# Transposing u in two row groups of 64 tokens, each into its own PSUM bank

## The chip, the cores and the metric

The kernel runs on one core of a Trainium2 chip. The metric is the device time of one execution in microseconds (us); lower is better. Three executions of the kernel before took 1543.83, 1544.32 and 1544.84 us, so the median is 1544.32 us. The core has five engines that run side by side, each through its own queue in order: TensorE (PE in the profile; its weight loads have a row of their own, PEld), VectorE (DVE), ScalarE (ACT), GpSimd (POOL) and SyncE (SP), which here only issues DMAs. TensorE writes its results to PSUM, which the kernel uses as eight banks of 128 partitions by 512 float32 numbers: four banks hold two tiles `ph` of 128 x 1024, and four more are handed out one by one as `px`.

## The reference

An attention through 49 agents is followed by a feed-forward block with SoLU and a layer norm. The second stage takes nearly all of the time:

```python
a2k = sm(agents, k); agent_v = a2k @ v        # per batch, 4 batches of 12608 tokens, 128 channels
x = sm(q, agents) @ agent_v                   # (50432, 128)
h = x @ w_in                                  # (50432, 1024)
e = exp(h - max(h)); sm = e / (sum(e) + 1e-9)
solu = h * sm
ln = (solu - mean(solu)) / sqrt(var(solu) + 1e-6) * g_ln
out = ln @ w_out                              # (50432, 128)
```

## The kernel before

**Tiles.** The tokens go through in n = 396 tiles of 128 (x counts them, 99 to a batch), in groups G of four. For each tile the kernel computes h for 128 tokens x 1024 features in `ph` (`c_h`, line 756, four matmuls: two feature halves, each with a high and a low part of the combined weights), its maximum over the features on VectorE (`c_max`, line 760), the exponential on ScalarE (`c_exp`, line 770), and u = h * exp on VectorE (`c_u`, line 775). ScalarE also sums the squares (`c_sq`, line 781) for the variance. The scale of a token is worked out on GpSimd, sent round through DRAM and multiplied in at the very end (`c_rstd`, `c_fin`).

**The turn.** The second matrix product needs u with features on the partitions, so TensorE transposes it. `c_t` (line 784) does it in two calls to a tile, one for each half of the features (hf = 0, 1), and each takes one px bank: four transposes of a 128 x 128 block (u is the loaded operand, the identity the streamed one) fill 128 features x 512 numbers. The names in the profile are `px<-ident,u`. `c_ev` (line 799) evicts each half on ScalarE: into `uT` in SBUF, or, for the halves that `DIR` names (`direct`), straight into the rounded high part `uH`. From uT, GpSimd makes uH (`c_sph`, line 814) and the low rest `uL` (`c_spl`, line 818), with one instruction over 1024 columns where neither half is direct, and over 512 where one is. For a direct half VectorE makes uL from the bank itself (`c_ldir`, line 809), and the bank comes free after that.

**The second product.** `c_w` (line 836) takes two tiles together (256 tokens): 24 matmuls of 256 columns accumulate in half a px bank, three for each of the eight feature blocks kf (wH with uH, wH with uL, wL with uH). One bank holds two such pairs until `c_fin` reads it. The first matmuls, up to half of the 24, waited for the parts of the first feature half only, those behind for both.

**Side stages.** Each batch begins with the agents' attention over the keys (`phase_a`), and every eighth tile with the queries' (`phase_b`). Some of their matmuls fill only 64 of the array's columns: lines 427 and 476 (`phase_a`) and 656 (`phase_b`) write to px partitions 0 to 63 and 64 to 127 in turns. Line 500 has an operand of one row.

**The order.** At build time a planner (`Plan.run`) places every operation in a list schedule: each has an engine, a booked cost, a due time and what it depends on. An operation with `take` can only start when a px bank is free by the plan; the one named by `free` gives it back. On TensorE the table `SWITCH` books a cost between kinds of operations: kind 2 are the ones with 64 columns, 0 the large products, 1 the rest. The order in which the planner calls the operations is the order of each engine's instructions. On the chip an engine goes through that order and waits by semaphores, so the booked costs do not set the time, but they set the order. Due times such as DT, DEV, DLD, DSP and DW (lines 177 to 181) are constants, counted in tiles.

Of the kernel before, what the change touches and what calls it, by code (L numbers as in the profile page):

```python
# [9 lines left out]
F32 = mybir.dt.float32  # L10
# [4 lines left out]
ALU = mybir.AluOpType  # L15
# [10 lines left out]
class Plan:  # L26
# [5 lines left out]
           "AA": 0.0, "AG": 0.17, "GP": 0.25 + MARGIN, "GD": 0.1, "GG": 0.1, "GA": 0.2}  # L32
    EPS = {"P": 0.01, "A": 0, "D": 0.07, "G": 2.6, "S": 0.0}

    SWITCH = ((0.0, 0.0, 0.09), (0.0, 0.0, 0.09), (0.15, 0.12, 0.0))

    HOLD = 0.12

# [7 lines left out]
    def op(self, eng, fn, cost, due, deps=(), take=False, free=None, after=(), kind=1, shy=0.0):  # L46
        o = Op()
        o.kind, o.shy = kind, shy
        o.eng, o.fn, o.cost, o.due, o.take, o.free = eng, fn, cost, due, take, free
        o.deps, o.outs, o.end, o.bank = [d for d in deps if d is not None], [], None, None  # L50
        o.left = 0
        for d in o.deps + [d for d in after if d is not None]:
            if d.end is None:
                o.left += 1
                d.outs.append(o)
        if not o.left:
            self.push(o)
        return o
# [7 lines left out]
    def run(self, idle=None):  # L66
        while True:
            best = None
            for e, ops in self.cand.items():
                if not ops:  # L70
                    continue
                free = [b[0] for b in self.banks if b[0] is not None]
                first = min(free) if free else None
                at, opts, low = self.at[e], [], None
                for o in ops:
                    s = max(at, o.ready[e])
                    if o.take:
                        if first is None:
                            continue
                        s = max(s, first)  # L80
                    opts.append((s, o))
                    low = s if low is None else min(low, s)
                if low is None:
                    continue
                near = [z for z in opts if z[0] <= low + self.EPS[e]]
                if e == "P" and self.kind == 2:
                    near = [z for z in opts if z[0] <= low + self.HOLD and z[1].kind == 2] or near
                s, o = min(near, key=lambda z: z[1].due)
                if o.shy > 0.0:
                    s, o = min((z for z in opts if z[0] <= s + o.shy), key=lambda z: z[1].due)  # L90
                if best is None or s < best[0]:
                    best = (s, e, o)
            if best is None:
                break
            s, e, o = best
            for z in o.eng:
                self.cand[z].remove(o)
            if o.take:
                can = [b for b in self.banks if b[0] is not None and b[0] <= s]
                bank = max(can, key=lambda b: b[0])  # L100
                bank[0], o.bank = None, bank
            if idle is not None and e == "P":
                idle(s - self.at[e])
            o.start, o.by = s, e
            if e == "S":
                hold, size, lag = o.cost
                self.at[e] = s + hold
                if size:
                    self.dma = max(self.dma, s + 2.0) + size / 0.36
                    o.end = self.dma + 0.3  # L110
                else:
                    o.end = s + lag
            else:
                c = o.cost[o.eng.index(e)] if len(o.eng) > 1 else o.cost
                if e == "P":
                    c += self.SWITCH[self.kind][o.kind]
                    self.kind = o.kind
                o.end = self.at[e] = s + c
            if o.free is not None:
                o.free.bank[0] = o.end + self.LAT[e + "P"]  # L120
            if o.fn:
                args = [o.bank[1]] if o.take else []
                if len(o.eng) > 1:
                    args.append(e)
                o.fn(*args)
            for z in o.outs:
                z.left -= 1
                if not z.left:
                    self.push(z)
# [3 lines left out]
def kernel(  # L133
# [11 lines left out]
    nc = tc.nc  # L145
# [3 lines left out]
    P = 128  # L149
    NF = DF // P  # L150
# [5 lines left out]
    AP2 = 64  # L156
# [3 lines left out]
    DIR = {(1, 0), (1, 1), (3, 1), (5, 1), (7, 1)}  # L160
    LGC = 8
    UB = 8
    TD = 2
    WC = 4

# [11 lines left out]
    DT = -0.42  # L177
    DEV = 5.19
    DLD = 0.41
# [601 lines left out]
        nc.scalar.activation(out=sq, in_=u, func=AF.Square, bias=su, scale=-float(DF),  # L781
                             accum_out=st[G]["Q"][:, j : j + 1])

    def c_t(x, hf, pt):
        rr[x, hf] = pt
        for kf in range(4):
            k0 = hf * 4 + kf
            nc.tensor.transpose(pt[:, kf * P : (kf + 1) * P], us[x][0][:, k0 * P : (k0 + 1) * P], ident)  # L788

    def direct(x, hf):  # L790
        return (x % (2 * GT), hf) in DIR or x >= n - TD

    def parts(x, k0, k1):
        i, j = divmod(x, 2)
        if i not in pr:
            pr[i] = [gpool.tile([P, NF, 2 * P], F32R, tag=t, name=f"{t}{x}") for t in ("uH", "uL")]
        return [t[:, k0:k1, j * P : (j + 1) * P] for t in pr[i]]

    def c_ev(x, hf):
        uH, _ = parts(x, hf * 4, hf * 4 + 4)  # L800
        pt = rr[x, hf].rearrange("p (k t) -> p k t", t=P)
        if direct(x, hf):
            nc.scalar.copy(out=uH, in_=pt)  # L803
        else:
            if x not in rr:
                rr[x] = epool.tile([P, NF, P], F32, tag="uT", bufs=UTB, name=f"uT{x}")
            nc.scalar.copy(out=rr[x][:, hf * 4 : hf * 4 + 4, :], in_=pt)  # L807

    def c_ldir(x, hf):
        uH, uL = parts(x, hf * 4, hf * 4 + 4)  # L810
        pt = rr[x, hf].rearrange("p (k t) -> p k t", t=P)
        nc.vector.tensor_tensor(out=uL, in0=pt, in1=uH.bitcast(F32), op=ALU.subtract)  # L812

    def c_sph(x, k0, k1):
        uH, _ = parts(x, k0, k1)
        nc.gpsimd.tensor_scalar(out=uH, in0=rr[x][:, k0:k1, :], scalar1=1.0, scalar2=0.0, op0=ALU.mult, op1=ALU.add)  # L816

    def c_spl(x, k0, k1):
        uH, uL = parts(x, k0, k1)
        nc.gpsimd.tensor_tensor(out=uL, in0=rr[x][:, k0:k1, :], in1=uH.bitcast(F32), op=ALU.subtract)  # L820

    WM = 3 * NF

# [95 lines left out]
    def F(f, *x):  # L919
        return lambda *y: f(*x, *y)  # L920
# [30 lines left out]
    def at(x, d, r, l):  # L951
        return x + d + (r * (1.0 - x / 12.0) if x < 12 else l if x >= (B - 1) * TB else 0.0)
# [4 lines left out]
    for x in range(n):  # L957
# [18 lines left out]
        if len(dh) < 2:  # L976
            utl.append(x)
            if len(utl) > UTB:
                buf.append(SP[utl[-1 - UTB]])
            if len(utl) <= UTB:  # L980
                buf += wready if (len(utl) + 2) % UTB == 2 else cout
        for hf in range(2):
            T[x, hf] = op("P", F(c_t, x, hf), 0.435, at(x, DT, DTR, DTL) + 0.02 * hf, [U[x]] + buf, take=True)
            EV[x, hf] = op("A", F(c_ev, x, hf), 0.477, at(x, DEV, DEVR, DEVL) + 0.02 * hf, [T[x, hf]],
                           free=None if hf in dh else T[x, hf])
            if hf in dh:
                LD[x, hf] = op("D", F(c_ldir, x, hf), 0.602, at(x, DLD, DLDR, DLDL), [EV[x, hf]], free=T[x, hf])
        need = [[LD.get((x, hf)), EV[x, hf]] for hf in range(2)]
        if len(dh) < 2:
            k0, k1 = (4 if 0 in dh else 0), (4 if 1 in dh else NF)  # L990
            SH[x] = op("G", F(c_sph, x, k0, k1), 0.17 + 0.107 * (k1 - k0), at(x, DSP, DSPR, DSPL),
                       [EV[x, hf] for hf in range(2) if hf not in dh])
            SP[x] = op("G", F(c_spl, x, k0, k1), 0.16 + 0.268 * (k1 - k0), at(x, DSP, DSPR, DSPL) + 0.02, [SH[x]])
            for hf in range(2):
                if hf not in dh:
                    need[hf] += [SH[x], SP[x]]
        else:
            SP[x] = None
        need_prev = need if x % 2 == 0 else [need_prev[hf] + need[hf] for hf in range(2)]
        if x % 2 == 1:  # L1000
            prev = None
            for m0 in range(0, WM, WC):
                m1 = min(m0 + WC, WM)
                lead = m0 == 0 and (i % 2 == 0 or i == n // 2 - 1)
                f = (lambda px, i=i, m1=m1: c_w(i, 0, m1, px)) if lead else F(c_w, i, m0, m1)
                o = op("P", f, 0.1192 * (m1 - m0), at(x, DW, DWR, DWL) + 2.0 * m0 / WM,
                       need_prev[0] + (need_prev[1] if m1 > WM // 2 else []) + wready + [prev, W.get((i - 1, 1)), FIN.get(G - 2)], take=lead, kind=0)
                if lead:
                    pol.append(o)
                prev = o  # L1010
            W[i, 1] = prev
# [75 lines left out]
```

## Time and profile before

| | |
|---|---|
| executions, us | 1543.83, 1544.32, 1544.84 |
| median, us | 1544.32 |
| profiled execution, us | 1545.92 |
| its span, first to last instruction, us | 1544.1 |
| instructions in the trace | 35,508 |
| granted TensorE clock, mean | 0.995 |
| HBM traffic, GB/s over the span | 85 |

The profile is that of one execution. Its page has the busy time of each engine, the chain of work that ended last, and the costliest groups of instructions; views of the trace give single instructions in order of time. In a group's row stand the line of the kernel, the engine, the operation, output and inputs by name, their shapes and the number of instructions, then the busy time in us, the mean time of one in ns, and the idle time of the engine before them. The span covers all but 1.8 us of the profiled execution, and that execution was 1.6 us over the median of the three.

### The profile page before, as it was taken

To read this page: it belongs to the slowest core of one execution; us is meant where nothing else is said; L and a number is where in the kernel's file an instruction comes from. 1 tells how busy PE (TensorE), PEld (TensorE's weight loads), DVE (VectorE), ACT (ScalarE), POOL (GpSimd) and SP (SyncE) were. 2 spreads that over 40 slices of the span, in tenths; PEclk is the share of its full clock that TensorE was granted. 3 is DMA by queue.
4 is the path that set the end of the run, shared out by engine and by line. 5 is a ranking of instruction groups with operands and counts; after the bars stand their busy time and mean duration, and the time that the engine had idled before them with its cause. 6 is when DMAs were issued, how large, how long until landed. Compare 5 with 4: busy or idle time off the path is not lost.

```text
span 1544.1 us, 35508 instructions
## 1 busy us (share of the span) xinstructions
PE 1514.7 (98%) x12624; PEld 1356.7 (88%) x12624; DVE 1373.8 (89%) x2213; ACT 1421.5 (92%) x2739; POOL 1256.1 (81%) x1613
## 2 busy tenths in 40 slices
PE   8799999999999999999999999999999999999998
PEld 5589898898898888999898998989999999999988
DVE  6889988898999888998989988888989989999896
ACT  3589999999999999999999999999999999999996
POOL 1478888788887888778877798888888989998986
PEclk9999999999999999999999999999999999999999
DMA  9533323333324342423234332432232323231211
GB/s 373 171 111 116 122 85 112 106 87 108 92 72 152 104 121 90 139 80 106 83 93 133 105 122 85 127 99 91 81 90 59 85 69 90 71 88 54 63 56 46
DMA packets 114720, 159.65 MB, mean 103 GB/s; under 512 B 16240, under 2 KB 71152, under 8 KB 114544
## 3 DMA queue, kind: packets, MB, share of 16 engines
q1 hardware_dynamic: 114544, 157.39, 32.9%
q8 instruction: 100, 1.64, 0.4%
q14 instruction: 76, 0.62, 0.1%
HBM read 105.36 MB, written 26.02 MB: 85 GB/s over the span
## 4 chain that ended last, share of the span: by engine, by line
PE 71%; ACT 9%; DVE 8%; POOL 5%; issue 4%; DMA 2%; SPq 0%; DVEq 0%; ACTq 0%; POOLq 0%
PE px L836 27%; PE ph L756 18%; PE px L788 16%; ACT e L770 3%; PE px L476 2%; DVE u L775 2%; PE px L427 2%; ACT sq L781 2%; POOL uL L820 2%; PE px L656 2%; ACT uT L807 2%; DVE nm L760 1%; DMA pT<-pn 1%; POOL uH L816 1%; PE px L460 1%
## 5 line engine op out<-in xcount | busy, mean ns | idle before, releaser
L820 POOL TENSOR_TENSOR uL<-uT,uH 128x1024 fp32r<-128x1024 f32 (+1 forms) x344 | 662.4, 1926 | 25.4
L760 DVE TENSOR_REDUCE nm<-ph 128x1 f32<-128x1024 f32 x396 | 479.5, 1216 | 69.2 <-PE ph L756 67.7
L775 DVE SCALAR_TENSOR_TENSOR u<-ph,e 128x1024 f32<-128x1024 f32 x396 | 481.1, 1219 | 38.3 <-ACT e L770 27.1
L781 ACT ACTIVATE sq<-u,su 128x1024 bf16<-128x1024 f32 x396 | 463.2, 1170 | 29.8 <-DVE u L775 22.2
L770 ACT ACTIVATE e<-ph,nm 128x1024 f32<-128x1024 f32 x396 | 448.8, 1137 | 19.2 <-DVE nm L760 18.0
L836 PE MATMUL px<-uL,wH 128*128 128x256 f32 x1584 | 462.8, 292 | 0.0
L836 PE MATMUL px<-uH,wH 128*128 128x256 f32 x1584 | 451.1, 285 | 2.6 <-ACT uT L807 1.3
L836 PE MATMUL px<-uH,wL 128*128 128x256 f32 x1584 | 449.8, 284 | 0.0
L788 PE MATMUL px<-ident,u 128*128 128x128 f32 x3168 | 431.5, 274 | 8.5 <-DVE u L775 7.4
L788 PEld LDWEIGHTS px<-ident,u 128*128 128x128 f32 x3168 | 366.2, 141 | 45.2 <-DVE u L775 7.2
L756 PE MATMUL ph<-mh,pT 128*128 128x512 f32 x792 | 335.3, 423 | 5.2 <-DMA pT<-pn 2.8
L816 POOL TENSOR_SCALAR uH<-uT 128x1024 fp32r<-128x1024 f32 (+1 forms) x344 | 299.9, 872 | 32.3 <-ACT uT L807 30.2
L756 PE MATMUL ph<-ml,pT 128*128 128x512 f32 x792 | 313.8, 396 | 0.2 <-DVE ml L552 0.2
L836 PEld LDWEIGHTS px<-uH,wH 128*128 128x128 f32 x1584 | 299.0, 189 | 16.1 <-issue 4.2
L807 ACT COPY uT<-px 128x512 f32<-128x512 f32 x541 | 301.8, 593 | 11.6 <-PE px L788 3.7
L836 PEld LDWEIGHTS px<-uL,wH 128*128 128x128 f32 x1584 | 298.9, 189 | 6.5 <-issue 2.8
L836 PEld LDWEIGHTS px<-uH,wL 128*128 128x128 f32 x1584 | 299.1, 189 | 5.5 <-issue 1.2
L812 DVE TENSOR_TENSOR uL<-px,uH 128x512 fp32r<-128x512 f32 x251 | 168.3, 684 | 17.5 <-ACT uH L803 16.9
L756 PEld LDWEIGHTS ph<-mh,pT 128*128 128x128 f32 x792 | 149.9, 189 | 33.4 <-issue 8.6
L756 PEld LDWEIGHTS ph<-ml,pT 128*128 128x128 f32 x792 | 150.7, 190 | 16.5 <-DVE ml L552 0.6
L803 ACT CAST uH<-px 128x512 fp32r<-128x512 f32 x251 | 147.0, 604 | 1.5 <-PE px L788 1.2
L855 POOL TENSOR_TENSOR y<-x,nhalf 128x4 f32<-128x4 f32 x99 | 100.2, 1013 | 7.7
(118 smaller groups left out, 1351.3 us busy)
## 6 DMA issues: line engine op xcount, KB each, us to landing
pT<-pn SPq DMA_DIRECT2D x392, 64.0 KB
rB<-dr SPq DMA_DIRECT2D x98, 256.0 KB
qt<-in_qT_dram SPq DMA_DIRECT2D x48, 512.0 KB
out_dram<-ob SPq DMA_DIRECT2D x95, 256.0 KB
kt<-in_kT_dram SPq DMA_DIRECT2D x36, 512.0 KB
vt<-in_v_dram SPq DMA_DIRECT2D x36, 512.0 KB
dr<-yr SPq DMA_DIRECT2D x392, 0.5 KB
kh<-in_kT_dram SPq DMA_DIRECT2D x12, 512.0 KB
```

Of the source, the lines that this page charges most:

```text
L756: nc.tensor.matmul(ph[:, sl], lhs, bmats[b]["mh" if m == 0 else "ml"][:, sl], start=(m == 0), stop=(m == 1))
L760: nc.vector.tensor_reduce(out=nms[x], in_=phs[x], op=ALU.max, axis=AX.X, negate=True)
L770: nc.scalar.activation(out=es[x], in_=phs[x], func=AF.Exp, bias=nms.pop(x), accum_out=st[G]["S"][:, j : j + 1])
L775: nc.vector.scalar_tensor_tensor(out=u, in0=phs[x], scalar=INV, in1=es[x], op0=ALU.mult, op1=ALU.mult, accum_out=su)
L781: nc.scalar.activation(out=sq, in_=u, func=AF.Square, bias=su, scale=-float(DF), accum_out=st[G]["Q"][:, j : j + 1])
L788: nc.tensor.transpose(pt[:, kf * P : (kf + 1) * P], us[x][0][:, k0 * P : (k0 + 1) * P], ident)
L803: nc.scalar.copy(out=uH, in_=pt)
L807: nc.scalar.copy(out=rr[x][:, hf * 4 : hf * 4 + 4, :], in_=pt)
L812: nc.vector.tensor_tensor(out=uL, in0=pt, in1=uH.bitcast(F32), op=ALU.subtract)
L816: nc.gpsimd.tensor_scalar(out=uH, in0=rr[x][:, k0:k1, :], scalar1=1.0, scalar2=0.0, op0=ALU.mult, op1=ALU.add)
L820: nc.gpsimd.tensor_tensor(out=uL, in0=rr[x][:, k0:k1, :], in1=uH.bitcast(F32), op=ALU.subtract)
L836: nc.tensor.matmul(po, wt[:, kf, :], ut[:, kf, :], start=(q == 0), stop=(q == WM - 1))
```

## The change

The two calls of `c_t` become one that takes two px banks. It transposes 64 tokens at a time: for each of the eight feature blocks it issues two transposes of 64 rows x 128 columns, one from partitions 0 to 63 of u into bank 0 and one from partitions 64 to 127 into bank 1, in turns. Each bank then holds all 1024 features (eight blocks of 128 on the partitions) for 64 tokens, so `hf` and `th` now number halves of the tokens. Eviction, the direct low part and GpSimd's split go by token halves: they write rows of 64 numbers, eight to an instruction of 512, where they wrote four rows of 128. The product needs all features of both tiles from its first matmul, and for that all of both token halves. The planner learns to take several banks for one operation, gets a kind 3 for the turn with 0.1 us at each change to and from it, and books 0.6 us for the 16 transposes, where it booked 0.435 us for each four. Due times are as before.

```diff
-    SWITCH = ((0.0, 0.0, 0.09), (0.0, 0.0, 0.09), (0.15, 0.12, 0.0))
+    SWITCH = ((0.0, 0.0, 0.09, 0.1), (0.0, 0.0, 0.09, 0.1), (0.15, 0.12, 0.0, 0.1), (0.15, 0.12, 0.1, 0.0))
...
-                free = [b[0] for b in self.banks if b[0] is not None]
-                first = min(free) if free else None
+                free = sorted(b[0] for b in self.banks if b[0] is not None)
...
                     if o.take:
-                        if first is None:
+                        if len(free) < o.take:
                             continue
-                        s = max(s, first)
+                        s = max(s, free[o.take - 1])
...
+    TCOST = 0.6
...
-    def c_t(x, hf, pt):
-        rr[x, hf] = pt
-        for kf in range(4):
-            k0 = hf * 4 + kf
-            nc.tensor.transpose(pt[:, kf * P : (kf + 1) * P], us[x][0][:, k0 * P : (k0 + 1) * P], ident)
+    def c_t(x, *pts):
+        u = us[x][0]
+        for th in range(2):
+            rr[x, th] = pts[th]
+        for k in range(NF):
+            for th in range(2):
+                rows = slice(th * AP2, (th + 1) * AP2)
+                nc.tensor.transpose(pts[th][:, k * AP2 : (k + 1) * AP2], u[rows, k * P : (k + 1) * P], ident[rows, rows])
...
-    def parts(x, k0, k1):
+    def parts(x, t0, t1):
...
-        return [t[:, k0:k1, j * P : (j + 1) * P] for t in pr[i]]
+        o = j * P + t0 * AP2
+        return [t[:, :, o : o + (t1 - t0) * AP2] for t in pr[i]]
...
-            nc.scalar.copy(out=rr[x][:, hf * 4 : hf * 4 + 4, :], in_=pt)
+            nc.scalar.copy(out=rr[x][:, :, th * AP2 : (th + 1) * AP2], in_=pt)
...
+        T[x, 0] = T[x, 1] = op("P", F(c_t, x), TCOST, at(x, DT, DTR, DTL), [U[x]] + buf, take=2, kind=3)
         for hf in range(2):
-            T[x, hf] = op("P", F(c_t, x, hf), 0.435, at(x, DT, DTR, DTL) + 0.02 * hf, [U[x]] + buf, take=True)
             EV[x, hf] = op("A", F(c_ev, x, hf), 0.477, at(x, DEV, DEVR, DEVL) + 0.02 * hf, [T[x, hf]],
-                           free=None if hf in dh else T[x, hf])
+                           free=None if hf in dh else (T[x, hf], hf))
...
                 o = op("P", f, 0.1192 * (m1 - m0), at(x, DW, DWR, DWL) + 2.0 * m0 / WM,
-                       need_prev[0] + (need_prev[1] if m1 > WM // 2 else []) + wready + [prev, W.get((i - 1, 1)), FIN.get(G - 2)], take=lead, kind=0)
+                       need_prev[0] + need_prev[1] + wready + [prev, W.get((i - 1, 1)), FIN.get(G - 2)], take=lead, kind=0)
```

`c_sph`, `c_spl` and `c_ldir` change in the same way as `c_ev`: `[:, k0:k1, :]` becomes `[:, :, t0 * 64 : t1 * 64]`. The tiles, their sizes, the four px banks and `DIR` stay.

More of the change, by code (lines that the diff above doesn't have):

```diff
@@ L99, in run @@
                 can = [b for b in self.banks if b[0] is not None and b[0] <= s]
-                bank = max(can, key=lambda b: b[0])
-                bank[0], o.bank = None, bank
+                o.bank = sorted(can, key=lambda b: -b[0])[: int(o.take)]
+                for b in o.bank:
+                    b[0] = None
             if idle is not None and e == "P":
@@ L119, in run @@
             if o.free is not None:
-                o.free.bank[0] = o.end + self.LAT[e + "P"]
+                of, i = o.free if isinstance(o.free, tuple) else (o.free, 0)
+                of.bank[i][0] = o.end + self.LAT[e + "P"]
             if o.fn:
-                args = [o.bank[1]] if o.take else []
+                args = [b[1] for b in o.bank] if o.take else []
                 if len(o.eng) > 1:
@@ L796, in parts, with c_ev @@
             pr[i] = [gpool.tile([P, NF, 2 * P], F32R, tag=t, name=f"{t}{x}") for t in ("uH", "uL")]
-        return [t[:, k0:k1, j * P : (j + 1) * P] for t in pr[i]]
[L799 to L802, printed above, removed]
+        o = j * P + t0 * AP2
+        return [t[:, :, o : o + (t1 - t0) * AP2] for t in pr[i]]
+    def c_ev(x, th):
+        uH, _ = parts(x, th, th + 1)
+        pt = rr[x, th].rearrange("p (k t) -> p k t", t=AP2)
+        if direct(x, th):
             nc.scalar.copy(out=uH, in_=pt)
@@ L806, in c_ev, with c_ldir, c_sph, c_spl @@
                 rr[x] = epool.tile([P, NF, P], F32, tag="uT", bufs=UTB, name=f"uT{x}")
[L807 to L811, printed above, removed]
+            nc.scalar.copy(out=rr[x][:, :, th * AP2 : (th + 1) * AP2], in_=pt)
+    def c_ldir(x, th):
+        uH, uL = parts(x, th, th + 1)
+        pt = rr[x, th].rearrange("p (k t) -> p k t", t=AP2)
         nc.vector.tensor_tensor(out=uL, in0=pt, in1=uH.bitcast(F32), op=ALU.subtract)
[L814 to L820, printed above, removed]
+    def c_sph(x, t0, t1):
+        uH, _ = parts(x, t0, t1)
+        nc.gpsimd.tensor_scalar(out=uH, in0=rr[x][:, :, t0 * AP2 : t1 * AP2], scalar1=1.0, scalar2=0.0, op0=ALU.mult, op1=ALU.add)
+    def c_spl(x, t0, t1):
+        uH, uL = parts(x, t0, t1)
+        nc.gpsimd.tensor_tensor(out=uL, in0=rr[x][:, :, t0 * AP2 : t1 * AP2], in1=uH.bitcast(F32), op=ALU.subtract)
     WM = 3 * NF
@@ L981 @@
                 buf += wready if (len(utl) + 2) % UTB == 2 else cout
+        T[x, 0] = T[x, 1] = op("P", F(c_t, x), TCOST, at(x, DT, DTR, DTL), [U[x]] + buf, take=2, kind=3)
         for hf in range(2):
-            T[x, hf] = op("P", F(c_t, x, hf), 0.435, at(x, DT, DTR, DTL) + 0.02 * hf, [U[x]] + buf, take=True)
             EV[x, hf] = op("A", F(c_ev, x, hf), 0.477, at(x, DEV, DEVR, DEVL) + 0.02 * hf, [T[x, hf]],
-                           free=None if hf in dh else T[x, hf])
+                           free=None if hf in dh else (T[x, hf], hf))
             if hf in dh:
-                LD[x, hf] = op("D", F(c_ldir, x, hf), 0.602, at(x, DLD, DLDR, DLDL), [EV[x, hf]], free=T[x, hf])
+                LD[x, hf] = op("D", F(c_ldir, x, hf), 0.602, at(x, DLD, DLDR, DLDL), [EV[x, hf]], free=(T[x, hf], hf))
         need = [[LD.get((x, hf)), EV[x, hf]] for hf in range(2)]
         if len(dh) < 2:
-            k0, k1 = (4 if 0 in dh else 0), (4 if 1 in dh else NF)
-            SH[x] = op("G", F(c_sph, x, k0, k1), 0.17 + 0.107 * (k1 - k0), at(x, DSP, DSPR, DSPL),
+            t0, t1 = (1 if 0 in dh else 0), (1 if 1 in dh else 2)
+            k0, k1 = 4 * t0, 4 * t1
+            SH[x] = op("G", F(c_sph, x, t0, t1), 0.17 + 0.107 * (k1 - k0), at(x, DSP, DSPR, DSPL),
                        [EV[x, hf] for hf in range(2) if hf not in dh])
-            SP[x] = op("G", F(c_spl, x, k0, k1), 0.16 + 0.268 * (k1 - k0), at(x, DSP, DSPR, DSPL) + 0.02, [SH[x]])
+            SP[x] = op("G", F(c_spl, x, t0, t1), 0.16 + 0.268 * (k1 - k0), at(x, DSP, DSPR, DSPL) + 0.02, [SH[x]])
             for hf in range(2):
```

## The prediction

> **What bounds the kernel now.** I read the page first (busy times, the chain of what ended last, the groups by shape), then the busy time in the steady stretch.
>
> ```profile
> span 1544.1 us, 35508 instructions
> PE 1514.7 (98%) x12624; PEld 1356.7 (88%) x12624; DVE 1373.8 (89%) x2213; ACT 1421.5 (92%) x2739; POOL 1256.1 (81%) x1613
> PE 71%; ACT 9%; DVE 8%; POOL 5%; issue 4%; DMA 2%; SPq 0%; DVEq 0%; ACTq 0%; POOLq 0%
> PE px L836 27%; PE ph L756 18%; PE px L788 16%; ACT e L770 3%; PE px L476 2%; DVE u L775 2%; PE px L427 2%; ACT sq L781 2%; POOL uL L820 2%; PE px L656 2%; ACT uT L807 2%; DVE nm L760 1%; DMA pT<-pn 1%; POOL uH L816 1%; PE px L460 1%
> ```
> ```profile
> 100.00:1500.00 1400.00, 1390.27 (x11603) 1260.90 (x11602) 1264.67 (x2010) 1335.92 (x2561) 1182.49 (x1515) 1.00 0.32 96
> ```
>
> The second fence has, for 100 to 1500 us, the busy time of PE, PEld, DVE, ACT and POOL, the granted clock (1.00), the DMA share and GB/s. TensorE is idle for 1400 - 1390.27 = 9.7 us there and leads the chain. ScalarE is next with 1335.92 us, so however much TensorE gains, this stretch cannot shrink by more than about 64 us. The turn (L788) is 16% of the chain.
>
> Busy says little of how densely matmuls follow each other, since each record includes the tail of its pipeline. So I take the pace from starts, in order of time on PE:
>
> ```profile
> 700.02 0.28 PE L836 MATMUL px<-uH,wL 128*128 128x256 f32 x1
> 700.13 0.28 PE L836 MATMUL px<-uH,wH 128*128 128x256 f32 x1
> 700.25 1.04 PE L788 MATMUL px<-ident,u 128*128 128x128 f32 x8
> 701.04 0.36 PE L836 MATMUL px<-uL,wH 128*128 128x256 f32 x1
> 701.24 0.28 PE L836 MATMUL px<-uH,wL 128*128 128x256 f32 x1
> 701.36 0.28 PE L836 MATMUL px<-uH,wH 128*128 128x256 f32 x1
> ```
> ```profile
> L788 PE MATMUL px<-ident,u 128*128 128x128 f32 x3168 | 431.5, 274 | 8.5 <-DVE u L775 7.4 <-ACT uT L807 0.5 <-DVE uL L812 0.4
> L656 PE MATMUL px<-ag_sb,qt 128*64 128x49 f32 x1584 | 57.4, 226 | 0.0
> ```
>
> A product step takes 0.117 us (701.24 to 701.36). The eight transposes last 1.04 us and the last one 0.274, so they are (1.04 - 0.274)/7 = 0.109 us apart. Check: from 700.13 to 701.24 are two product steps (0.234) and the turn: 1.11 - 0.234 = 0.876, against 8 x 0.109 = 0.872 us. The turn goes in and out without a loss, and 396 tiles cost 396 x 0.872 = 345 us of TensorE.
>
> **The change part by part.** *16 transposes of half the rows.* The trace has none of 64 rows. What it has are pairs that fill half of the columns each, in turns, and the cost of changing the array's shape:
>
> ```profile
> 840.97 1.09 PE L656 MATMUL px<-ag_sb,qt 128*64 128x49 f32 x32
> ```
> ```profile
> 509.49 0.39 PE L756 MATMUL ph<-ml,pT 128*128 128x512 f32 x1
> 509.80 1.09 PE L476 MATMUL px<-vt,eT 128*64 128x128 f32 x16
> 510.73 1.03 PE L427 MATMUL px<-kt,ag_sb 128*64 128x512 f32 x4
> 511.69 0.39 PE L836 MATMUL px<-uH,wH 128*128 128x256 f32 x1
> 511.91 0.28 PE L836 MATMUL px<-uL,wH 128*128 128x256 f32 x1
> 512.03 0.28 PE L836 MATMUL px<-uH,wL 128*128 128x256 f32 x1
> ```
> ```profile
> L427 PE MATMUL px<-kt,ag_sb 128*64 128x512 f32 x144 | 37.5, 599 | 0.0
> ```
> ```profile
> 394.48 0.19 PEld L476 LDWEIGHTS px<-vt,eT 64*64 64x64 f32 x2 [0.17 <-issue]
> 394.84 0.19 PEld L476 LDWEIGHTS px<-vt,eT 128*64 128x64 f32 x2 [0.17 <-issue]
> ```
>
> The 32 matmuls of L656 go as 16 pairs: (1.09 - 0.226)/15 = 0.058 us to a pair, with two loads of 64 columns in it. Eight pairs of L476, which stream 128 columns, take from 509.80 to 510.73: 0.93 with a first load, so some 0.11 a pair. Two halves of the array thus cost the time of one. I call the step of a pair of half-row transposes p. Its streamed part is 64 columns, half of a transpose's: 0.055 us by proportion. Its loads:
>
> ```profile
> L788 PE MATMUL px<-ident,u x1: 327/327/327, 842.0 to 842.0; 128*128 128x128 f32 x1
> ```
> ```profile
> L836 PE MATMUL px<-uH,wH x1: 385/385/385, 511.7 to 511.7; 128*128 128x256 f32 x1
> L836 PE MATMUL px<-uH,wH x1584: 276/281/394, 82.2 to 1537.8; 128*128 128x256 f32 x198
> ```
>
> These are durations in ns (least/median/most) of one line's instructions. The L788 row and the first L836 row are one matmul each, right after a change of shape, where nothing hides the load. The transpose takes 327 where the mean is 274: its load costs 0.053 us. A product matmul takes 385 against 281: 0.104. So p is bounded below by 0.055 (load and stream alike). It is 0.058 if row groups go side by side as the column groups of L656 do; 0.11 if the two loads, or the two streams, take turns. I take 0.058, the nearest row, a pair with loads of like price.
>
> *The change of shape*, twice a turn. From the product step at 509.49 to the second at 511.91 there are 2.42 us, in which stream 0.234 (the 509.49 step: two feature halves of L756 are 0.23 apart), 8 x 0.109, two pairs of L427 and 0.117. Of L427's four the last lasts 0.599, so the second pair comes 1.03 - 0.599 = 0.43 after the first: in all 0.234 + 0.872 + 0.86 + 0.117 = 2.08. The rest, 0.34 us, is what the excursion costs: array emptied, first load uncovered, and both again on the way back. It is not the columns alone: between the two loads above only the number of rows changes (64, then 128), and 0.36 - 2 x 0.109 = 0.14 us is lost for one change, its small load included; 0.14 in and, with the dearer product load (0.104 for 0.053), 0.19 out is 0.33. I take 0.34, with none at all as the low end.
>
> The Trainium skill speaks to this twice. "TensorE: Matmul & The Clock Gate", section "LDWEIGHTS (loading the stationary operand)", has the time of a load go with its columns, at 107 ns for 128, and not with its rows: halving rows would halve no load, and double their number; an estimate from its figure, loads side by side, is 0.34 + 0.05 + 8 x 0.107 = 1.25 us a turn. The uncovered product load (0.104) agrees, the transposing one (0.053) does not; what a half-row load costs no row shows. "TensorEngine Tiling (Array Packing)", section "Key Properties", lets different tiles load and multiply in parallel; by it p would be 0.058, and L656 agrees for column groups alone.
>
> Sum per tile: before 0.872; after 0.34 + 8 x 0.058 = 0.80; 0.07 saved. With 0.007 for the second group of the last pair, 0.06: 396 x 0.06 = 24 us. Ends with the 0.34: p = 0.055 saves 0.872 - 0.78 = 0.09, or 36 us; p = 0.11 costs 0.34 + 0.88 - 0.872 = 0.35 more, or 138 us. The balance lies at p = (0.872 - 0.34)/8 = 0.066.
>
> *Two banks at once, eviction after all 16.* ScalarE could start on the first half 0.44 us after the turn began; now after about 0.7, with 0.59 us for each eviction:
>
> ```profile
> L807 ACT COPY uT<-px 128x512 f32<-128x512 f32 x541 | 301.8, 593 | 11.6 <-PE px L788 3.7 <-POOL uH L816 2.8 <-issue 1.6
> ```
> ```profile
> 704.59 0.60 PE L788 MATMUL px<-ident,u 128*128 128x128 f32 x4
> 704.95 0.47 PE L756 MATMUL ph<-mh,pT 128*128 128x512 f32 x1
> 705.26 0.40 PE L756 MATMUL ph<-ml,pT 128*128 128x512 f32 x1
> 705.50 0.60 PE L788 MATMUL px<-ident,u 128*128 128x128 f32 x4
> ```
>
> Here the plan let the first half go and put a product before the second, 0.55 us: that goes. A turn must now find two of four banks free together, while one holds the second product nearly always. Behind a turn that waits, PE's queue holds the next `c_h` and product steps, and DVE's maximum waits for `c_h`. What covers it is that the planner puts ready products in front. Uncovered, it costs at most an eviction (0.59) a tile, 234 us; covered, nothing. Since all of TensorE's idle time is 9.7 us over some 360 tiles, I take about a third of that in addition, 4 us.
>
> *The product needs all halves.* It starts later in a pair's life; no work is added, and 24 matmuls of an older pair cover it. Nothing, or a share of the same wait.
>
> *Rows of 64 numbers* in eviction, uL and the split:
>
> ```profile
> L812 DVE TENSOR_TENSOR uL<-px,uH 128x512 fp32r<-128x512 f32 x251 | 168.3, 684 | 17.5 <-ACT uH L803 16.9
> L668 DVE TENSOR_TENSOR logits<-px,mx 128x392 f32<-128x392 f32 x48 | 26.8, 561 | 0.6
> ```
>
> L668 writes rows of 49: 561 ns for 392 numbers against 684 for 512, (684 - 561)/120 = 1.03 ns each, so 157 ns of fixed cost in both. Short rows cost DVE nothing. For ScalarE and GpSimd I take nothing too; 5% more on ScalarE's 0.59 would be 396 x 2 x 0.03 = 24 us of ScalarE, inside its 64 us.
>
> No DMA is added or removed, and no step changes its engine.
>
> The sum: -24 + 4 = -20 us. The profiled execution took 1545.9 (span 1544.1 and 1.8 around it), 1.6 above the median; from the median: 1544.3 - 20 = **1524 us**.
>
> **The rivals.**
> 1. *Row groups take turns* (slower). The half-row loads or streams don't run together: p = 0.11, +138 us, **1682**. For it: no pair of row groups is in the trace. Against: column groups run in pairs. It decides from p = 0.066 on. In the same direction: side by side, but each half-row load at a plain load's 0.104: p = 0.11 and 0.05 more at the start, +158, 1702. For it: the load that follows rows, not this operation; against it the 327 ns. Chances 0.12 and 0.04.
> 2. *Waits for two banks* (slower or equal). TensorE stands still for an eviction in more than one tile of ten (0.06/0.59) and the 24 us are gone; in one of six, 396 x 0.59/6 = 39 us, less 24: +15, **1559**. Against: TensorE hardly waits now. Chance 0.14.
> 3. *No price for the change of shape.* Turn 0.47, -160 us on TensorE, then ScalarE binds: at most -64, about **1490**. Against: the 0.14 us between two loads that differ in rows alone. Chance 0.08.
> 4. *It doesn't do what it says*: 64-row pairs as dear as one transpose with p at 0.066 by some fixed cost. Within 3 us, 1544. Chance 0.07.
>
> **How the numbers follow.** The forecast (p 0.055 to 0.064, little waiting: -36 to -5 us) has 0.55. 0.2% is 3 us, about what a measurement of this kernel can tell from no change. Faster: 0.55 + 0.08 and 0.01 of rival 4's fringe: 0.64. Same: 0.06 of rival 4 and 0.03 of rival 2: 0.09. Slower: 0.12 + 0.04 + 0.11 = 0.27. The range leaves out rival 1 (0.16) and a little of 3: 1490 to 1560; the likeliest case alone has 1508 to 1540.
>
> **What would show it.** In time order a turn is 16 matmuls of 64 rows; from the product step before it to the second after it should lie 0.234 + 0.81 = 1.04 us (now 1.11). A pair step of 0.11 means rival 1; the first product matmul behind a turn at 281 instead of 385 ns, rival 3; TensorE idle far over 9.7 us from 100 to 1500, with a px release named by the turn, rival 2. L807, L803, L812, L816 and L820 should keep their durations. I would be wrong most plainly if half-row pairs don't overlap.

## The result, and the profile after

The changed kernel takes **1590.62 us** (median of four executions, 1589.04 to 1593.73). The kernel before, on the same chip, took 1544.58. The ratio is 1.0292, with a 95% interval of 1.0277 to 1.0307: 46 us slower (1590.62 - 1544.58), where 20 us faster was forecast, and above the range's end of 1560.

The head of the page after, and its chain of waits, which covers only the last few instructions here (all shares round to 0%) and so can't be read as that of before was:

```profile
span 1589.5 us, 42120 instructions
...
PE 1516.6 (95%) x15792; PEld 1251.8 (79%) x15792; DVE 1378.5 (87%) x2217; ACT 1420.7 (89%) x2735; POOL 1253.0 (79%) x1613
...
PE 0%; DVE 0%; issue 0%
```

The busy time from 100 to 1500 us after (PE, PEld, DVE, ACT, POOL, clock, DMA share, GB/s):

```profile
100.00:1500.00 1400.00, 1353.36 (x14246) 1127.73 (x14245) 1233.53 (x1967) 1297.12 (x2489) 1144.41 (x1472) 0.99 0.31 95
```

TensorE is idle for 1400 - 1353.36 = 46.6 us there, 9.7 before, and no other engine has taken over: the others are all less busy in these 1400 us than before. Over the whole span TensorE's idle time is 1589.5 - 1516.6 = 72.9 us; it was 1544.1 - 1514.7 = 29.4. So 43.5 of the 46 us are plain standing still.

The granted clock is not quite as before (0.99 for 1.00). In these 1400 us it fell to half in four short spells, together 17.0 us, where the kernel before had one of 3.4 us (770.8 to 774.2):

```profile
721.90:728.70 6.80, 5.78 (x54) 4.01 (x54) 5.00 (x12) 4.59 (x10) 2.60 (x8) 0.50 0.70 169
762.90:766.30 3.40, 3.40 (x23) 2.35 (x22) 3.16 (x6) 3.37 (x7) 3.32 (x3) 0.50 0.44 101
930.10:933.50 3.40, 3.40 (x23) 2.16 (x23) 2.58 (x5) 2.00 (x4) 2.01 (x6) 0.51 0.68 204
1268.10:1271.50 3.40, 3.40 (x20) 2.70 (x16) 2.33 (x5) 3.30 (x8) 3.32 (x3) 0.50 0.58 154
```

Each of them follows or overlaps one or two waits of TensorE of 0.8 to 1.8 us (the one before follows a wait of 1.4 us). Inside them the matmuls of `c_h` start 0.43 us apart (1269.58, 1270.01), elsewhere 0.23 (705.59, 705.82). TensorE is busy for 15.98 us in the four, for 3.40 in the one before, so by estimate (15.98 - 3.40) x (1 - 0.23/0.43) = 5.9, some 6 us, are lost by the slower clock.

**The turn did get shorter.** TensorE in order of time after (start, duration, instruction), one turn between two product steps:

```profile
701.27 0.28 PE L842 MATMUL px<-uL,wH 128*128 128x256 f32 x1
701.48 0.71 PE L793 MATMUL px<-ident,u 64*128 64x64 f32 x16
702.12 0.38 PE L842 MATMUL px<-uH,wL 128*128 128x256 f32 x1
702.35 0.28 PE L842 MATMUL px<-uH,wH 128*128 128x256 f32 x1
```

From the product step before the turn to the second after it are 702.35 - 701.27 = 1.08 us; 1.04 was forecast and 1.11 it was. Less two product steps (0.234) that is 0.846 us. Over all the turns that stand between products in the trace, the median is 0.836 us, against 0.875 before. The turn saves 0.039 us on 396 tiles, 15 us, where 24 were forecast. Inside it, the instructions of line 793 whose records begin in two short windows (least/median/most duration in ns, first and last start):

```profile
L793 PE MATMUL px<-ident,u x2: 272/273/274, 701.5 to 701.5; 64*128 64x64 f32 x2
...
L793 PE MATMUL px<-ident,u x10: 222/222/223, 701.7 to 702.0; 64*128 64x64 f32 x10
```
```profile
701.48 0.28 PE L793 MATMUL px<-ident,u 64*128 64x64 f32 x2
...
701.72 0.47 PE L793 MATMUL px<-ident,u 64*128 64x64 f32 x10
```

The first two, one of each row group, last 272 to 274 ns each and 0.28 us together: they start within 10 ns of each other. The last ten are five pairs in 0.47 us, of which the last lasts 0.222: four pair steps take 0.248 us, 0.062 a pair. The rest of the turn is 0.836 - 8 x 0.062 = 0.34 us for the excursion.

**The bill.** The kernel is 46 us slower although the turn saves 15, so some 61 us have come in: 43.5 as idle time in the profile, and the other 17 inside the busy time, which rose (1516.6 against 1514.7) although the turns in it shrank by 15. Some 6 of the 17 are the slower clock. The rest are probably waits too short to show behind the tails of the matmul records; that is argued from the sum and not seen one by one.

The groups that were to keep their durations, of before and after:

```profile
L820 POOL TENSOR_TENSOR uL<-uT,uH 128x1024 fp32r<-128x1024 f32 (+1 forms) x344 | 662.4, 1926 | 25.4
...
L816 POOL TENSOR_SCALAR uH<-uT 128x1024 fp32r<-128x1024 f32 (+1 forms) x344 | 299.9, 872 | 32.3 <-ACT uT L807 30.2
...
L803 ACT CAST uH<-px 128x512 fp32r<-128x512 f32 x251 | 147.0, 604 | 1.5 <-PE px L788 1.2
```
```profile
L826 POOL TENSOR_TENSOR uL<-uT,uH 128x1024 fp32r<-128x1024 f32 (+1 forms) x344 | 661.0, 1922 | 25.9
...
L822 POOL TENSOR_SCALAR uH<-uT 128x1024 fp32r<-128x1024 f32 (+1 forms) x344 | 298.8, 869 | 73.8 <-ACT uT L813 73.2
...
L813 ACT COPY uT<-px 128x512 f32<-128x512 f32 x541 | 299.7, 592 | 19.5 <-PE px L793 7.1
...
L818 DVE TENSOR_TENSOR uL<-px,uH 128x512 fp32r<-128x512 f32 x251 | 168.0, 684 | 23.5 <-ACT uH L809 22.9
...
L809 ACT CAST uH<-px 128x512 fp32r<-128x512 f32 x251 | 145.6, 604 | 1.4 <-PE px L793 1.4
```

Means of 1922, 869, 592, 684 and 604 ns against 1926, 872, 593, 684 and 604: rows of 64 numbers cost nothing on any engine. What did change stands at the ends of the rows: GpSimd waits 73.2 us for evictions, 30.2 before. Three other waits, before and then after (who waits, for whom: us in total, times, longest):

```profile
DVE u L775 <- ACT e L770: 27.1, 81, 1.3
...
DVE u L775 <- PE px L788: 5.9, 10, 1.2
```
```profile
DVE u L777 <- ACT e L772: 57.0, 102, 1.8
...
DVE u L777 <- PE px L793: 24.1, 35, 1.5
...
PE ph L758 <- DVE u L777: 17.3, 29, 1.8
```

The third is what TensorE pays: the first product `c_h` wants the `ph` tile that `c_u` frees. Its group, before and after:

```profile
L756 PE MATMUL ph<-mh,pT 128*128 128x512 f32 x792 | 335.3, 423 | 5.2 <-DMA pT<-pn 2.8 <-issue 1.6 <-DVE u L775 0.4
```
```profile
L758 PE MATMUL ph<-mh,pT 128*128 128x512 f32 x792 | 346.1, 437 | 18.9 <-DVE u L777 17.3 <-issue 0.6 <-DMA pT<-pn 0.5
L793 PE MATMUL px<-ident,u 64*128 64x64 f32 x6336 | 283.1, 229 | 19.4 <-DVE u L777 8.5 <-DVE pn L704 3.5 <-ACT uT L813 3.3
```

0.4 us for u has become 17.3. The turn's idle time (L793) has grown too, from 8.5 to 19.4 us, but not by its wait for u. Of that, 7.4 us stood there before, in three waits with the same longest one. The rest, 10.9 us where there were 1.1, ends with instructions that read a px bank and so give it back (`pn`, `uT`, `uL` and others). Before, and then after:

```profile
PE px L788 <- DVE u L775: 7.4, 3, 3.8
```
```profile
PE px L793 <- DVE u L777: 8.5, 3, 3.8
...
PE px L793 <- DVE pn L704: 3.5, 4, 1.3
...
PE px L793 <- ACT uT L813: 3.3, 5, 0.9
```

One wait of `c_h` for u as it stands in the order of time, on TensorE, VectorE and ScalarE after:

```profile
705.82 0.39 PE L758 MATMUL ph<-ml,pT 128*128 128x512 f32 x1
706.75 0.50 PE L758 MATMUL ph<-mh,pT 128*128 128x512 f32 x1 [0.54 <-DVE u L777]
```
```profile
705.46 1.23 DVE L777 SCALAR_TENSOR_TENSOR u<-ph,e 128x1024 f32<-128x1024 f32 x1 [0.84 <-ACT e L772]
```

```profile
703.25 1.06 ACT L813 COPY uT<-px 128x512 f32<-128x512 f32 x2
704.20 1.14 ACT L772 ACTIVATE e<-ph,nm 128x1024 f32<-128x1024 f32 x1
```

`c_u` (705.46) waited 0.84 us for the exponential, and on ScalarE that one stands right behind the two evictions of a turn. In ScalarE's order these now come together more often: one stands alone 72 times in the trace, 179 times before. TensorE goes through its queue in order, so it stands still for 0.54 us.

### The profile page after: what moved, and what is told of

It is laid out like the page before. It is cut to its first block, busy times and chain, and to the rows that moved or that the text cites. A ratio compares the mean times of both kernels' runs of the same rounds, so it can differ in the third digit from the quotient of the medians.

```text
span 1589.5 us, 42120 instructions
## 1 busy us (share of the span) xinstructions
PE 1516.6 (95%) x15792; PEld 1251.8 (79%) x15792; DVE 1378.5 (87%) x2217; ACT 1420.7 (89%) x2735; POOL 1253.0 (79%) x1613
## 5 line engine op out<-in xcount | busy, mean ns | idle before, releaser
L826 POOL TENSOR_TENSOR uL<-uT,uH 128x1024 fp32r<-128x1024 f32 (+1 forms) x344 | 661.0, 1922 | 25.9
L842 PE MATMUL px<-uL,wH 128*128 128x256 f32 x1584 | 450.4, 284 | 1.2 <-POOL uL L826 1.1
L758 PE MATMUL ph<-mh,pT 128*128 128x512 f32 x792 | 346.1, 437 | 18.9 <-DVE u L777 17.3
L822 POOL TENSOR_SCALAR uH<-uT 128x1024 fp32r<-128x1024 f32 (+1 forms) x344 | 298.8, 869 | 73.8 <-ACT uT L813 73.2
L793 PEld LDWEIGHTS px<-ident,u 64*128 64x128 f32 x6336 | 228.6, 139 | 114.8 <-issue 30.7
L842 PEld LDWEIGHTS px<-uH,wL 128*128 128x128 f32 x1584 | 299.1, 189 | 10.9 <-issue 1.9
L793 PE MATMUL px<-ident,u 64*128 64x64 f32 x6336 | 283.1, 229 | 19.4 <-DVE u L777 8.5
L758 PEld LDWEIGHTS ph<-ml,pT 128*128 128x128 f32 x792 | 151.5, 191 | 17.3 <-DVE ml L554 0.6
```

The costliest lines, as they stand in the source:

```text
L758: nc.tensor.matmul(ph[:, sl], lhs, bmats[b]["mh" if m == 0 else "ml"][:, sl], start=(m == 0), stop=(m == 1))
L793: nc.tensor.transpose(pts[th][:, k * AP2 : (k + 1) * AP2], u[rows, k * P : (k + 1) * P], ident[rows, rows])
L822: nc.gpsimd.tensor_scalar(out=uH, in0=rr[x][:, :, t0 * AP2 : t1 * AP2], scalar1=1.0, scalar2=0.0, op0=ALU.mult, op1=ALU.add)
L826: nc.gpsimd.tensor_tensor(out=uL, in0=rr[x][:, :, t0 * AP2 : t1 * AP2], in1=uH.bitcast(F32), op=ALU.subtract)
L842: nc.tensor.matmul(po, wt[:, kf, :], ut[:, kf, :], start=(q == 0), stop=(q == WM - 1))
```

## The experiments

At the start there were two theories of the 61 us. That of the **order**: two banks at once, given back late, leave the planner less room. That of the **rows**: something in the half-row work is dearer than its records show. The first is told apart into its parts below. Each ratio is to the kernel before, run beside it; 0.001 is 1.5 us.

**The order of after without the half-row work.** Eight full transposes in place of 16, feature halves in place of token halves; bookings, banks and order as in the changed kernel.

```diff
-            for th in range(2):
-                rows = slice(th * AP2, (th + 1) * AP2)
-                nc.tensor.transpose(pts[th][:, k * AP2 : (k + 1) * AP2], u[rows, k * P : (k + 1) * P], ident[rows, rows])
+            nc.tensor.transpose(pts[k // 4][:, k % 4 * P : (k % 4 + 1) * P], u[:, k * P : (k + 1) * P], ident)
...
```

> The changed kernel's order of operations, its bookings and its two banks at a time are kept; only the turn itself is undone: eight transposes of 128 x 128 into the two banks, eviction and split by feature halves as before. Theory W (the order that two banks at once force on the planner makes TensorE wait, some 62 us of new waits): stays near the changed kernel's 1590.6, plus up to 14 us, since a turn costs 0.872 instead of 0.836 us: 1585 to 1605. Theory R (the half-row work itself is dear: change of shape, short rows): back to about 1545. Theory F (due times fitted to the old durations and structure): as W here.

Measured: 1597.95 us, 1.0338 (1.0308 to 1.0369). The slowdown is all there without one half-row instruction, so the theory of the rows falls. The row-group turn is worth 1.0338 - 1.0292 = 0.0046, 7 us (2 to 12 by the two intervals), in this order: about half of the 15 us. That fits an order in which TensorE waits for something else, so that a shorter turn in part only lengthens the wait, but it is not shown.

**Two banks at once, late eviction, on the kernel before** (full transposes, booked at 0.87 us; in this and the next kernel the queries' transposes also wait for an older stage).

```diff
+        T[x, 0] = T[x, 1] = op("P", F(c_t, x), 0.87, at(x, DT, DTR, DTL), [U[x]] + buf, take=2)
         for hf in range(2):
-            T[x, hf] = op("P", F(c_t, x, hf), 0.435, at(x, DT, DTR, DTL) + 0.02 * hf, [U[x]] + buf, take=True)
...
```

> The kernel before with one part of the change alone: the two halves of the turn become one operation that takes two banks at once, with full-width transposes at their old cost (0.87), old feature halves, and no kind 3; evictions only after all eight. (The query stage's transposes also take their bank only when their result can be evicted, else the plan finds no end.) Theory W: slower by 40 us or more, 1585 or above, with TensorE idle by tens of us from 100 to 1500 us (9.7 before). Theory R: 1545 within 5. Theory F: some 10 to 30 us above 1545, as for any disturbance.

**Two banks at once, early eviction**: the first four transposes take both banks, and the first half may be evicted, and something else put in, before the second four.

```diff
+        T[x, 0] = op("P", F(c_t, x, 0), 0.435, at(x, DT, DTR, DTL), [U[x]] + buf, take=2)
+        T[x, 1] = op("P", F(c_t, x, 1), 0.435, at(x, DT, DTR, DTL) + 0.02, [T[x, 0]])
...
```

> As the run with two banks at once, but the turn stays two operations of four transposes: the first takes both banks, and its half can be evicted while the second is still turned or even waits. If the late eviction (both halves only after the whole turn) is the larger part of theory W: under half of the loss of the run with the single operation, 1545 to 1570. If taking two banks at once is all of it: the same loss, 1585 or above. Theory R: 1545.

Measured: 1610.43 us, 1.0427 (1.0386 to 1.0468), and 1566.93 us, 1.0138 (1.0108 to 1.0168). Busy time from 100 to 1500 us, late and then early:

```profile
100.00:1500.00 1400.00, 1354.66 (x11191) 1211.91 (x11187) 1214.94 (x1941) 1278.12 (x2449) 1129.61 (x1453) 1.00 0.31 94
```
```profile
100.00:1500.00 1400.00, 1380.41 (x11458) 1249.29 (x11459) 1249.88 (x1990) 1315.85 (x2528) 1164.40 (x1498) 1.00 0.31 95
```

TensorE is idle 45.3 us with late eviction, nearly as in the changed kernel (46.6), and 19.6 with early. Against the 1543.85 us of the kernel before beside them, the late kernel loses 67 us; 44 of these go when the first half can be evicted early, and two banks at once are left with 23.

**A due time alone.** How much does the order lose when nothing but a due time is moved? Here the turn is due half a tile later.

```diff
-    DT = -0.42
+    DT = 0.08
```

> The kernel before with one due time moved by half a tile (DT from -0.42 to 0.08) and nothing else. Theory F (the due times are fitted so closely that any disturbance costs): slower by 10 us or more, 1555 to 1575. Theory W, where the loss needs the two banks: within 5 us of 1544.5. Theory R says the same.

Measured: 1575.91 us, 1.0199 (1.0168 to 1.0229), 32 us. So the 23 us above are no larger than what a due time that does not fit costs, and the 44 us not much larger: these runs make late eviction likely as the larger part, but do not part it from an order that its due times do not fit. The due times had been chosen for the order of before. Hence the next runs: the 42 due times searched anew for each structure, so that the planner's own plan ends early. One or two dependences were added in them that the new orders need.

```diff
-    TCOST = 0.6
+    TCOST = 0.64
...
-    DT = -0.42
-    DEV = 5.19
+    DT = -0.63
+    DEV = 0.75
...
-        SQ[x] = op("A", F(c_sq, x), 1.15, at(x, DSQ, DSQR, DSQL), [U[x]] + ([om] if not x else []))
+        SQ[x] = op("A", F(c_sq, x), 1.15, at(x, DSQ, DSQR, DSQL), [U[x]] + ([om] if x < 8 else []))
```

A second number came in with them, the planner's **reserve** (line 29). Every hand-over to TensorE from VectorE, ScalarE or GpSimd, a bank that comes free among them, is booked that much later than its latency:

```python
    MARGIN = 0.4
    LAT = {..., "DP": 0.26 + MARGIN, ..., "AP": 0.25 + MARGIN, ..., "GP": 0.25 + MARGIN, ...}
```

The changed kernel, refitted with reserves of 0.4, 0.2 and 0.05 us:

> The changed kernel with its 42 due times searched anew for its own structure (booked turn 0.64 instead of 0.6, from the 0.836 us measured between product steps; two orders added: the query stage's transposes take a bank only when their result can be evicted, and the first eight tiles' squares wait for the weights' mean). Theory F (the loss is only that the due times fitted the old structure): 1525 to 1540, below the kernel before, as a turn is 0.036 us shorter (396 x 0.036 = 14 us). Theory L (a late eviction holds two of four banks for the whole turn, whatever the order): better than 1590 but still above before, 1550 to 1570.

> As the refitted changed kernel, with the planner's reserve on the hand-over of a px bank (MARGIN) at 0.2 instead of 0.4 us, and the due times searched again with it. Theory L, with banks as what is scarce: a bank that counts as free 0.2 us earlier twice a tile makes room, so below the refit with 0.4, 1530 to 1550. Theory F: no difference to the refit with 0.4 beyond 5 us.

> As the run with a reserve of 0.2, with 0.05. Theory L: a little lower still, 1525 to 1545, if the real hand-over keeps to the booked one; if it doesn't, TensorE waits in order for banks that the plan counts free, and it is slower than with 0.2. Theory F: as with 0.4.

Early and late eviction with full transposes (the two kernels above), refitted with the reserve of 0.4; the late one also with 0.05:

> The run with two banks at once, full-width transposes and early eviction of the first half, its due times searched anew (reserve 0.4, the same two added orders). Theory L: taking two banks at once costs nothing by itself, so within 8 us of before, 1537 to 1553. If taking two banks at once is itself the loss: it stays at 1560 or above.

> The run with two banks at once (full-width transposes in one operation, evicted late, 1610), its due times searched anew with the reserve at 0.4. Theory L (late eviction costs by itself when banks are booked with 0.4 us of reserve): stays clearly above the one with early eviction (1539.8), 1555 to 1580. Theory F alone: within 5 us of that one.

> Full-width transposes, two banks at once, one operation and so late eviction, with the reserve at 0.05 and the due times searched anew: the refitted changed kernel with 0.05 but for the row groups. A turn costs 0.87 instead of 0.836 us: if TensorE binds in both, 10 to 20 us slower than that one's 1526.8, 1535 to 1548.

And the kernel before, refitted with 0.05, 0.4 and 0.2:

> The control: the kernel before, its turn and banks untouched, with the reserve at 0.05 and its due times searched as long as those of the changed kernel. If the row-group turn is worth its 14 us (396 x 0.036) once the order fits: slower than the refitted changed kernel with the same reserve (ratio to before 0.986), 1530 to 1545. If the later eviction takes that back, and what the refits gained is due to the search alone: as fast as that or faster, 1510 to 1528.

> The kernel before with the reserve as it was (0.4) and its due times searched anew as long as the others. If the order of before was at its best already: 1540 to 1547. If the search finds more for any structure: 1525 to 1538, and the gains of the refitted changed kernel are to be counted from here.

> The kernel before with the reserve at 0.2 and its due times searched anew, against the refitted changed kernel with 0.2 (ratio 0.9875 to before): the same reserve and the same length of search, only the turn and its banks differ. If the row-group turn pays once the order fits: slower, ratio 0.99 to 1.00. If its later eviction takes the gain back: 0.98 to 0.9875.

Measured, as ratios with their intervals, and the medians in us:

| structure, refitted | reserve 0.4 | reserve 0.2 | reserve 0.05 |
|---|---|---|---|
| before (one bank at a time) | 0.9849 (0.9836 to 0.9862), 1523.80 | 1.0033 (1.0020 to 1.0047), 1551.51 | 1.0001 (0.9989 to 1.0013), 1546.54 |
| two banks, early, full transposes | 0.9949 (0.9931 to 0.9966), 1539.79 | | |
| two banks, late, full transposes | 1.0202 (1.0187 to 1.0217), 1578.00 | | 0.9917 (0.9905 to 0.9929), 1534.27 |
| changed kernel (two banks, late, row groups) | 0.9974 (0.9964 to 0.9984), 1543.52 | 0.9875 (0.9859 to 0.9890), 1529.02 | 0.9862 (0.9847 to 0.9877), 1526.78 |

What follows. Two banks at once with early eviction, refitted, are faster than before (0.9949): taking two banks costs nothing in itself that due times can't mend. Other due times (with the turn booked at 0.64 and the two dependences added), at the reserve of 0.4, bring the changed kernel from 1.0292 to 0.9974, 0.0318 or 49 us. The late kernel with full transposes stays 2% slow at that reserve (1.0202), and the small one takes 0.0285, 44 us, off it. On the kernel before, the reserve goes the other way: 0.9849 with 0.4 and 1.0001 with 0.05.

The first of these runs missed what was expected, and so did the kernel before refitted with 0.4: its order had not been at its best, and 23 us lay in its due times. The kernel before refitted with 0.05 and with 0.2, the late one with 0.05 and the changed one with 0.2 also came out beside what was expected, by 1 to 5 us. With 0.2 the kernel before came out slower than with either end, and the two late kernels at 0.4 lie 0.0228, 35 us, apart, over twice what the turn saves. So a search leaves a scatter of its own, and steps of 0.02 between two refits are not to be read as the worth of a structure. That is why the reserve was then changed alone.

**The reserve alone, one number in each kernel**, due times as they were:

```diff
-    MARGIN = 0.4
+    MARGIN = 0.05
```

> The changed kernel with one number changed: the planner's reserve on the hand-over of a bank (MARGIN) 0.05 instead of 0.4 us; due times as they are. If the new waits come from the reserve on two banks at once, which makes the planner put the turn off and the real banks stand free meanwhile: most of the 46 us goes, 1540 to 1560. If they come from the due times alone: 1580 to 1595.

> The control: the kernel before with MARGIN 0.05 and nothing else. If the reserve matters for two banks at once alone: within 8 us of before (either way), with no gain. If a smaller reserve helps any structure: faster by 5 us or more, and the gain of the changed kernel with 0.05 is to be counted less that.

Measured: the changed kernel 1548.39 us, 1.0016 (1.0005 to 1.0027); the kernel before 1554.63 us, 1.0063 (1.0045 to 1.0082). One number takes 0.0276, 43 us, off the changed kernel, as expected there, and adds 10 us to the one before, where neither theory had it slower by more than 8. Busy time from 100 to 1500 us of the changed kernel with it, and the two groups of TensorE:

```profile
100.00:1500.00 1400.00, 1379.54 (x14634) 1154.05 (x14631) 1267.62 (x2016) 1331.27 (x2562) 1179.86 (x1513) 1.00 0.32 97
```
```profile
L758 PE MATMUL ph<-mh,pT 128*128 128x512 f32 x792 | 339.1, 428 | 6.6 <-DVE u L777 5.6 <-DMA pT<-pn 0.3 <-issue 0.2
L793 PE MATMUL px<-ident,u 64*128 64x64 f32 x6336 | 282.5, 229 | 11.5 <-DVE u L777 8.3 <-DVE uL L818 2.1 <-ACT uT L813 0.8
```

The idle time falls from 46.6 to 20.5 us; the wait of `c_h` for u, from 17.3 to 5.6; the turn's waits for others than u, from 10.9 to 3.2. The instructions are the same ones, the turn costs the same; only the order differs.

**The fastest.** The changed kernel refitted with 0.05 and the kernel before refitted with 0.4. The page and the busy time from 100 to 1500 us, first of the one, then of the other:

```profile
span 1524.4 us, 42058 instructions
...
PE 1494.4 (98%) x15794; PEld 1251.2 (82%) x15794; DVE 1371.8 (90%) x2216; ACT 1410.5 (93%) x2736; POOL 1257.2 (82%) x1613
```
```profile
100.00:1500.00 1400.00, 1388.65 (x14801) 1175.60 (x14797) 1277.09 (x2036) 1343.19 (x2593) 1202.14 (x1536) 1.00 0.32 97
```
```profile
span 1521.6 us, 35490 instructions
...
PE 1505.0 (99%) x12624; PEld 1355.0 (89%) x12624; DVE 1371.8 (90%) x2211; ACT 1416.4 (93%) x2741; POOL 1253.9 (82%) x1613
```
```profile
100.00:1500.00 1400.00, 1399.01 (x11705) 1276.12 (x11705) 1276.77 (x2024) 1347.31 (x2594) 1197.62 (x1538) 1.00 0.32 96
```

Both beat the two kernels of this case, and their intervals overlap (0.9862 and 0.9849). The row turn has 10.6 us less busy time on TensorE (1505.0 - 1494.4) and gives it back as idle time: 11.4 us in the 1400, against 1.0. Whether an order can be found that keeps both stays open. With due times as given, or at one and the same reserve, the answer differs: the row turn leads at 0.2 and 0.05, the old turn at 0.4.

## Why the prediction was wrong

**The step that failed** is "*Two banks at once, eviction after all 16*", as the prediction put it: "What covers it is that the planner puts ready products in front", and "I take about a third of that in addition, 4 us". Some 61 us came, nearly all of them waits (some 6 the slower clock beside them). The cover was argued from TensorE's idle time before, 9.7 us, and that belonged to an order in which a turn needed one bank, could be split in two (it was split around other work in about a third of the tiles), and had due times chosen for it. The planner with two banks to find, both evicted late and both booked with the reserve, made another order, and on the chip TensorE waits in it. The kernel with full transposes in the new order (1.0338) shows that no instruction's price has a part in it. Two edits of numbers, each by itself, take nearly all of it away: the reserve alone 43 us, other due times (with the turn booked at 0.64 and two dependences added) 49. So the waits are those of one order, not a toll on every turn. The reserve is no cause by itself either, since the same number makes the kernel before slower. In the three pairs of kernels with two banks held late that differ in it, 0.4 is the slower (1.0292 against 1.0016; refitted, 0.9974 against 0.9862 and 1.0202 against 0.9917), and in the two pairs with one bank at a time the faster (1.0000 against 1.0063, 0.9849 against 1.0001). The direction is the same in all five; the sizes contain the scatter of the orders. How much of the loss late eviction makes by itself, and how much any order would that its due times do not fit, stays open: a due time alone cost 32 us. The reserve sits on every hand-over to TensorE, so how much goes by the banks and how much by the other hand-overs (u to the turn, uH to the product) was not separated.

**Rival 2**, waits for two banks, was the right kind and was underrated twice: 0.14 as a chance, and +15 us as a price, from a guess of one tile in six. Of its marks, "TensorE idle far over 9.7 us" showed; the other, a px release named by the turn, showed as well: 10.9 us of the turn's idle time end with a reader of a px bank, 1.1 before. The largest single wait stands elsewhere, though, in `c_h` for u (17.3 us), which holds a `ph` tile and no px bank. So an order that banks have changed need not show its price where the banks are taken.

**The turn.** Going side by side, the price of the change of shape and the saving were forecast in the right direction, so rival 1 (0.11 a pair), the dear plain load and rival 3 (no price for the change) fall. The excursion was forecast at 0.34 and measured 0.34. The first product after a turn lasts 0.38 us as forecast, where its mean was 281 ns. The term that was off is p: 0.062 for 0.058 us, so 0.836 us a turn, not 0.80 to 0.81, and 15 us, not 24. With p so near to the balance of 0.066, an error of 0.004 was 8 x 0.004 x 396 = 13 us.

The Trainium skill, "TensorEngine Tiling (Array Packing)", section "Key Properties", lets different tiles load and multiply in parallel: the trace agrees for row groups too, two of which start within 10 ns. "TensorE: Matmul & The Clock Gate", section "LDWEIGHTS (loading the stationary operand)", has a load go with its columns, by its formula 107 ns for 128: by it the prediction had a turn of 1.25 us as an estimate, and the trace does not agree (0.836, with a pair of such loads every 62 ns).

**Rows of 64 numbers**: nothing, as forecast, within 4 ns on every engine. **The product needs all halves**: it was costed at nothing, and as the change also has it together with the late eviction, it was not measured apart. In the kernel of the experiments with two banks and late eviction, made from the kernel before, the first matmuls of the product still needed the first feature half only, and it lost 67 us, so the loss does not need it.

**Rival 4** does not hold: the change does what it says, and the turn is 0.039 us shorter.

## What to carry to other kernels

Where an order is planned at build time, an edit that changes what an operation holds (banks, buffers) and for how long is first a change of the order: price it by what a small displacement of that order costs (here 32 us for half a tile in one due time), not by the idle time of the old order, and expect more of it than of the instructions saved. Before such a change is judged, fit the planner's numbers to it and fit the old kernel as well, since here due times and reserve moved the kernels by 0.6 to 5%, while the shorter turn was 1% of TensorE's time and 0.5% of the kernel's where the order was kept. A booked reserve is no neutral safety: in the pairs measured here 0.4 us of it was better than 0.05 where one bank was held at a time and worse where two were held late.

## What was not expected of the hardware

A pair of half-row transposes, two loads of 64 x 128 and 64 streamed columns each, takes 0.062 us, slightly more than the 0.055 us of its streamed part by proportion and the 0.058 of a pair of half-column products. The sixteen loads of the turn shown above (least/median/most in ns):

```profile
L793 PEld LDWEIGHTS px<-ident,u x16: 135/138/140, 701.5 to 701.9; 64*128 64x128 f32 x16
```

The last starts at 701.9 and the first at 701.5, so some 0.5 to 0.6 us hold sixteen loads of 0.138 us: about four of them are open at a time in the records, and the duration of a load there is not its pace.
